# Keeping the gelu derivative of the last chunk in SBUF, and starting the FFN backward with that chunk

## The chip, the cores and the metric

The kernel runs on one core of a Trainium2 chip. Times are device microseconds (us) of one execution. A run is called slow when it took over 1.5% longer than the fastest run of the same kernel, otherwise fast.

A ratio is the mean time of one kernel's fast runs over that of the other's fast runs of the same rounds, so it isn't quite the ratio of the medians that stand beside it.

TensorE, VectorE, ScalarE, GpSimd and SyncE are PE, DVE, ACT, POOL and SP in the profile. PEld is TensorE's weight load. L12 is line 12 of the kernel, and the same statement has a number some 13 higher after the change.

## The reference

One transformer block and its gradients: 2048 tokens, width 512, FFN width 1792, 32 heads of 16 values. Attention looks at 8 positions, each 2 apart. Cut to what matters:

```python
h  = x + A_ref(layernorm(x), wqkv, wo)           # dilated window attention
h2 = h + gelu(layernorm(h) @ w1 + b1) @ w2 + b2  # tanh form of gelu
_out, _vjp = jax.vjp(_f, A_x, A_wqkv, A_wo, B_w1, B_b1, B_w2, B_b2)
return (_out, *_vjp(grad_out))                   # eight outputs
```

## The kernel before

The tokens are cut in four chunks of 512 (c = 0 to 3). The forward makes `u` (the input of gelu) and `s` (a sigmoid of it) in pairs of feature tiles, seven pairs a chunk, stores both to DRAM beside the result `g`, and the FFN backward loads them again to make the derivative `y`:

```python
# forward, for each chunk c and each of its seven pairs f2
z = ...; nc.scalar.activation(out=z[:], in_=u[:], func=ACT.Square)
...                                              # two VectorE operations on z
nc.scalar.activation(out=s[:], in_=z[:], func=ACT.Sigmoid, scale=2.0 * GC)
nc.vector.tensor_tensor(out=gt[:], in0=u[:], in1=s[:], op=ALU.mult)
for dd, t_ in ((x_d[c][r0:r1, :], u), (s_d[c][r0:r1, :], s), (g_d[...], gt)):
    pq.dma_start(out=dd.rearrange(...), in_=t_[:])      # pq is GpSimd's queue

# FFN backward of one chunk (b1_gg), for each pair
u = br2.tile(..., tag="bu", bufs=4); s = br2.tile(..., tag="bs", bufs=4)
...                                              # loads u and s on pq
nc.scalar.activation(out=y[:], in_=u[:], func=ACT.Square)
...                                              # five VectorE, one ScalarE operation: y
# psg = grad_out @ w2.T on TensorE; then gh = psg * y on VectorE
```

Behind the matmuls of one backward chunk runs the gradient of w2 as filler. Its transposed tiles `gtm` come from DRAM, 512 KB each, through two buffers.

`b_go(c)` turns the chunk's gradient through wo (TensorE, matmuls psgo), stores it as `go_r`, and `b_ga(c)` loads it as `go` and makes the gradient of the attention weights: products `pag` on VectorE, sums `ga` on TensorE, the results `gl` on VectorE. `b_sum` then makes the gradients of v, q and k from `r` (loads of `go_r`, `k_r` and `q_r`), with products `pb` on VectorE. Each engine gets its instructions in an order that is fixed when the kernel is built, and that isn't always the source's: in e2 below, loads of `r` go out at 506.1 us, before a store (527.2 us) that stands ahead of them in the source.

```python
for i in range(1, NC):                    # the i-th chunk of the backward
    ...                                   # b1_gg(i), with filler gw2
    if i == NC - 1:
        mix(b_go(0), none)
        b_ga(0)
    ...                                   # b1_gx(i), with filler gw2
    if i > 1:
        mix(b_go(i - 1), none)
b_ga(1)
mix(b_go(3), gw2)                         # the chunk that came last
...                                       # gb1r: the sum of grad b1, its store on SP
for c in range(NC):
    ...                                   # b_sum(c, 2), with filler grad w1
    if c + 2 < NC:
        b_ga(c + 2)
```

## Time and profile before

| | before |
|---|---|
| three runs known at first | 767.05, 771.17, 756.03 us |
| profiled execution: span, clock | 760.9 us, 0.937 |
| TensorE, VectorE, ScalarE, GpSimd busy | 83%, 73%, 52%, 29% |
| bytes moved by DMA | 170.91 MB |
| last g of the forward | 296.7 us |
| gb1r (FFN backward and grad w2 done) | 528.7 us |
| last gl (end of the last b_ga) | 597.3 us |

The last three rows are read from the view of one tile's instructions. It prints how often an instruction ran, its shortest, median and longest duration in ns, and the start of its first and last one in us. For the kernel before:

```profile
L784 DVE COPY gb1r<-ptg x1: 205/205/205, 528.7 to 528.7; 14x128 bf16<-14x128 bf16 x1
L731 DVE TENSOR_TENSOR gl<-attn,sp x8: 681/686/693, 517.2 to 597.3; 128x512 bf16<-128x512 bf16 x8
```

They are used as milestones: the same work must be done by then in every version. The remaining views of this kernel (busy times, stretches, waits, groups) stand in the prediction, with how to read them.

### The profile page before, as it was taken

To read this page: it belongs to the slowest core of one execution; us is meant where nothing else is said; L and a number is where in the kernel's file an instruction comes from. 1 tells how busy PE (TensorE), PEld (TensorE's weight loads), DVE (VectorE), ACT (ScalarE), POOL (GpSimd) and SP (SyncE) were. 2 spreads that over 40 slices of the span, in tenths; PEclk is the share of its full clock that TensorE was granted. 3 is DMA by queue.
4 is the path that set the end of the run, shared out by engine and by line. 5 is a ranking of instruction groups with operands and counts; after the bars stand their busy time and mean duration, and the time that the engine had idled before them with its cause. 6 is when DMAs were issued, how large, how long until landed. Compare 5 with 4: busy or idle time off the path is not lost. (4 is left out here: it accounts for less than half of the span.)

```text
span 760.9 us, 10214 instructions
## 1 busy us (share of the span) xinstructions
PE 629.8 (83%) x3552; PEld 263.9 (35%) x3618; DVE 556.3 (73%) x919; ACT 391.9 (52%) x545; POOL 219.5 (29%) x330
## 2 busy tenths in 40 slices
PE   2896478698795898966989898998898868999996
PEld 1441122233241333323444444443332323334342
DVE  5538879799758453563989898377988958898745
ACT  4662238759277374453778677552111323356443
POOL 4343333435244266441342433312101201000100
PEclk9997789699697899987999999999999989999999
DMA  8587897858677599999797785837987698975462
GB/s 222 167 296 201 225 332 249 292 201 270 245 218 238 150 251 273 272 244 146 161 207 160 192 190 146 254 104 242 400 236 286 189 335 280 327 260 175 154 124 69
DMA packets 112769, 170.91 MB, mean 225 GB/s; under 512 B 69549, under 2 KB 77582, under 8 KB 112718
## 3 DMA queue, kind: packets, MB, share of 16 engines
q1 hardware_dynamic: 80092, 79.45, 39.4%
q0 software_dynamic: 25856, 84.52, 35.0%
q10 hardware_dynamic: 6770, 6.30, 2.8%
q8 instruction: 28, 0.46, 0.3%
q14 instruction: 23, 0.19, 0.1%
HBM read 94.64 MB, written 60.38 MB: 204 GB/s over the span
## 5 line engine op out<-in xcount | busy, mean ns | idle before, releaser
L328 DVE TENSOR_TENSOR pb<-ba,r 128x2048 bf16<-128x2048 bf16 x96 | 112.3, 1220 | 15.2 <-PE pss L333 15.1
L631 PE MATMUL psw<-gout,gtm 128*128 128x512 bf16 x201 | 51.6, 391 | 22.1 <-DMA gtm<-g_d 11.5
L471 PE MATMUL psf<-ln2T,w 128*128 128x512 bf16 x217 | 57.5, 394 | 10.3 <-ACT u L473 9.4
L749 PE MATMUL psw<-h1tm,ln2a 128*128 128x512 bf16 (+1 forms) x248 | 54.6, 352 | 7.9 <-ACT ow L752 6.0
L494 PE MATMUL ps<-w,g 128*128 128x512 bf16 x217 | 54.6, 382 | 3.6 <-DVE g L481 3.4
L685 PE MATMUL psx<-w1T,gh 128*128 128x512 bf16 x214 | 51.3, 379 | 0.9 <-DVE luf L617 0.7
L664 DVE CUSTOM_DVE_ANT_0 gh<-psg,by 128x512 bf16<-128x512 f32 x54 | 36.1, 685 | 13.6 <-PE psg L662 11.9
L650 ACT ACTIVATE by<-bu 128x1024 bf16<-128x1024 bf16 x28 | 29.7, 1059 | 30.1 <-DVE gb1p L664 25.1
L311 DVE TENSOR_TENSOR pag<-go,bv 128x2048 bf16<-128x2048 bf16 x32 | 38.0, 1219 | 6.4 <-PE ga L318 3.4
L369 ACT CAST qkv<-psq 128x512 bf16<-128x512 f32 x48 | 27.6, 586 | 28.1 <-PE psq L367 28.1
L328 DVE TENSOR_TENSOR pbo<-a,v 128x2048 bf16<-128x2048 bf16 x32 | 38.1, 1216 | 5.3 <-DMA a<-at_r 4.2
L662 PE MATMUL psg<-goutT,w2T 128*128 128x512 bf16 x160 | 41.5, 379 | 0.6 <-DVE gb1p L664 0.2
L473 ACT ACTIVATE u<-psf,b1c 128x512 bf16<-128x512 f32 x56 | 36.4, 681 | 7.7 <-PE psf L471 3.4
L631 PEld LDWEIGHTS <-gtm 128*128 128x128 bf16 x208 | 20.4, 100 | 48.9 <-issue 15.8
L479 ACT ACTIVATE s<-z 128x1024 bf16<-128x1024 bf16 x28 | 29.4, 1058 | 14.4 <-DMA s_d<-s 8.6
L673 ACT COPY th<-pth 128x1024 bf16<-128x1024 bf16 x27 | 27.1, 1004 | 18.2 <-PE pth L671 15.1
L749 PEld LDWEIGHTS <-ln2a 128*128 128x128 bf16 x256 | 22.6, 97 | 36.9 <-issue 20.9
L675 POOL DMA_DIRECT2D h1tm_d<-th x27 | 20.6, 764 | 48.5 <-ACT th L673 46.7
L471 PEld LDWEIGHTS <-w 128*128 128x128 bf16 x224 | 20.7, 100 | 39.0 <-issue 20.8
L481 DVE TENSOR_TENSOR g<-u,s 128x1024 bf16<-128x1024 bf16 x28 | 19.1, 688 | 19.7 <-ACT s L479 19.7
L333 PE MATMUL pss<-pb,sel 128*32 128x512 bf16 x384 | 30.8, 389 | 2.6 <-DVE pb L328 2.4
L842 PE MATMUL psy<-wqkvT,gT 128*128 128x512 bf16 x125 | 32.0, 383 | 0.4
(196 smaller groups left out, 1340.8 us busy)
## 6 DMA issues: line engine op xcount, KB each, us to landing
v<-v_r SPq DMA_DIRECT2D x16, 576.0 KB, 7.7
r<-go_r SPq DMA_DIRECT2D x16, 576.0 KB, 8.6
r<-k_r SPq DMA_DIRECT2D x16, 576.0 KB, 8.3
r<-q_r SPq DMA_DIRECT2D x16, 576.0 KB, 4.9
x_d<-u POOLq DMA_DIRECT2D x28, 256.0 KB, 4.4
s_d<-s POOLq DMA_DIRECT2D x28, 256.0 KB, 4.7
g_d<-g POOLq DMA_DIRECT2D x28, 256.0 KB, 4.2
bu<-x_d POOLq DMA_DIRECT2D x28, 256.0 KB, 4.9
```

Of the source, the lines that this page charges most:

```text
L311: nc.vector.tensor_tensor(out=pr[:], in0=_ap(q_ap, [q_ap.ap[0], [P, 2], [0, W], [1, P]]), in1=_ap(k_ap, [k_ap.ap[0], [P, 2], [-DIL * P, W] ...
L328: last = nc.vector.tensor_tensor(out=pr[:], in0=_ap(a_ap, [a_ap.ap[0], [2 * H, CJ], [0, Q4], [1, H]], off=wh * H + (4 * H * wh if sg else 0)),
L333: mm = nc.tensor.matmul(ps[PR * n:PR * n + PR, :], lhsT=sel4[:], rhs=prs[wh][:, TC * n:TC * n + TC, :, :].rearrange("p j d h -> p (j d h)" ...
L471: nc.tensor.matmul(ps[:], lhsT=w1[0][:, dc, ft * P:(ft + 1) * P], rhs=ln2T[:, dc, :], start=(dc == 0), stop=(dc == DC - 1))
L473: nc.scalar.activation(out=u[:, i, :], in_=ps[:], func=ACT.Identity, bias=b1c[:, ft:ft + 1], scale=1.0)
L494: nc.tensor.matmul(ps[:], lhsT=gs[ft // 2][:, ft % 2, j * P:(j + 1) * P], rhs=w2[0][:, ft, :], start=(ft == 0), stop=False)
L631: nc.tensor.matmul(ps[:], lhsT=gtm[:, t, :], rhs=gout[t // TC][:, t % TC, :], start=(t == 0), stop=(t == NT - 1))
L662: nc.tensor.matmul(ps[:], lhsT=w2T[:, dc, ft * P:(ft + 1) * P], rhs=gT[:, dc, :], start=(dc == 0), stop=(dc == DC - 1))
L664: nc.vector.tensor_tensor_reduce(out=t1[:, k2, :], in0=ps[:], in1=y[:, k2, :], scale=1.0, scalar=0.0, op0=ALU.mult, op1=ALU.add, accum_out ...
L685: nc.tensor.matmul(ps[:], lhsT=t1s[ft // 2][:, ft % 2, j * P:(j + 1) * P], rhs=w1T[:, ft, :], start=(ft == 0), stop=(ft == FT - 1))
L749: nc.tensor.matmul(ps[:, 0:nf * P], lhsT=ln2a[:, t // TC, t % TC, dc * P:(dc + 1) * P], rhs=tmx[:, t, 0:nf * P], start=(t == 0), stop=(t = ...
L842: nc.tensor.matmul(ps[:], lhsT=gT[sel][:, g, j * P:(j + 1) * P], rhs=wqkvT[:, sel * G + g, :], start=(n == 0), stop=(n == NJ - 1))
```

## The change

The intent: the last chunk's `u` and `s` are still in SBUF at the end of the forward. If its `y` is made there and kept (in the buffers of `bu` and `bs`, seven of eight), that chunk's stores, loads and squares fall away, and its backward can begin at once. For that the backward must begin with chunk 3. The core of the diff:

```diff
+    def dgelu(y, u, s, t):        # five operations, as before in the backward
 ...
+            if c == 3:
+                tag = "bu" if f2 < 4 else "bs"
+                y = ys[f2] = br2.tile([P, 2, CH], BF16, name=f"y{c}_{f2}", tag=tag, bufs=4)
+                nc.vector.tensor_scalar(out=y[:], in0=z[:], scalar1=6.0 * GC * GK, scalar2=2.0 * GC, ...)
 ...
+            if c == 3:
+                dgelu(y, u, s, z)
-            for dd, t_ in ((x_d[c][r0:r1, :], u), (s_d[c][r0:r1, :], s), (g_d[...], gt)):
+            for dd, t_ in ((x_d[c][r0:r1, :], u), (s_d[c][r0:r1, :], s), (g_d[...], gt))[2 if c == 3 else 0:]:
 ...
-    b1_order = (0, 1, 2, 3)
+    b1_order = (3, 0, 1, 2)
 ...
+    ...                               # w1T_load and the set-up of the backward, moved up
+    mix(f_ffn1(3), f_ffn2(2))         # moved down behind them
 ...
+            if c in yc:
+                y = ...                   # the kept tile: no load, no chain
+            else:
                 ...                       # as before
 ...
         if i > 1:
-            mix(b_go(i - 1), none)
+            mix(b_go(3 if i == 2 else 1), none)
     b_ga(1)
-    mix(b_go(3), gw2)
+    mix(b_go(2), gw2)
```

Since y borrows buffers of the backward, the set-up of the backward (its pools, the first load of grad_out, the load of w1T) now stands ahead of the last forward chunk in the source. The order of `b_ga` (0, 1, 2, 3) is not changed.

More of the change, by code (lines that the diff above doesn't have):

```diff
@@ L459 @@
     GB = 12
-    gts = {}
+    gts, ys = {}, {}
+    def dgelu(y, u, s, t):
+        nc.vector.tensor_tensor(out=y[:], in0=y[:], in1=u[:], op=ALU.mult)
+        nc.scalar.activation(out=t[:], in_=s[:], func=ACT.Identity, bias=one_t[:], scale=-1.0)
+        nc.vector.tensor_tensor(out=y[:], in0=y[:], in1=t[:], op=ALU.mult)
+        nc.vector.tensor_scalar(out=y[:], in0=y[:], scalar1=1.0, scalar2=None, op0=ALU.add)
+        nc.vector.tensor_tensor(out=y[:], in0=y[:], in1=s[:], op=ALU.mult)
     def f_ffn1(c):
@@ L475, in f_ffn1 @@
             nc.scalar.activation(out=z[:], in_=u[:], func=ACT.Square)
+            if c == 3:
+                tag = "bu" if f2 < 4 else "bs"
+                y = ys[f2] = br2.tile([P, 2, CH], BF16, name=f"y{c}_{f2}", tag=tag, bufs=4)
+                nc.vector.tensor_scalar(out=y[:], in0=z[:], scalar1=6.0 * GC * GK, scalar2=2.0 * GC, op0=ALU.mult, op1=ALU.add)
             nc.vector.tensor_scalar(out=z[:], in0=z[:], scalar1=GK, scalar2=1.0, op0=ALU.mult, op1=ALU.add)
@@ L482, in f_ffn1 @@
             gts[c].append(gt)
+            if c == 3:
+                dgelu(y, u, s, z)
             r0, r1 = 2 * f2 * P, (2 * f2 + 2) * P
-            for dd, t_ in ((x_d[c][r0:r1, :], u), (s_d[c][r0:r1, :], s), (g_d[r0:r1, c * CH:(c + 1) * CH], gt)):
+            for dd, t_ in ((x_d[c][r0:r1, :], u), (s_d[c][r0:r1, :], s), (g_d[r0:r1, c * CH:(c + 1) * CH], gt))[2 if c == 3 else 0:]:
                 pq.dma_start(out=dd.rearrange("(i p) t -> p i t", p=P), in_=t_[:])
@@ L569 @@
     f_h(3)
-    mix(f_ffn1(3), f_ffn2(2))
     fr.release()
-    fl.release()
     br1 = pool("br1", 1, side="right")
-    b1_order = (0, 1, 2, 3)
+    b1_order = (3, 0, 1, 2)
     gout, goutT = {}, {}
@@ L599, in make_goutT @@
             to_T(gout[c], goutT[c], f"e{c}", "T")
+    w1T_load = sync.dma_start_transpose(out=w1T[:], in_=B_w1[:, :])
+    gate(w1T_load, ("r", 3))
+    mix(f_ffn1(3), f_ffn2(2))
+    fl.release()
     make_goutT(0)
-    gate(sync.dma_start_transpose(out=w1T[:], in_=B_w1[:, :]), ("r", 3))
     for c in b1_order[1:]:
@@ L643, in b1_gg @@
         for f2 in range(FT // 2):
-            u = br2.tile([P, 2, CH], BF16, name=f"bu{c}_{f2}", tag="bu", bufs=4)
-            s = br2.tile([P, 2, CH], BF16, name=f"bs{c}_{f2}", tag="bs", bufs=4)
-            for t_, d_t in ((u, x_d), (s, s_d)):
-                dd = d_t[c][2 * f2 * P:(2 * f2 + 2) * P, :]
-                pq.dma_start(out=t_[:], in_=dd.rearrange("(i p) t -> p i t", p=P))
-            y = br2.tile([P, 2, CH], BF16, name=f"by{c}_{f2}", tag="by", bufs=2)
-            mark["y", i, f2] = nc.scalar.activation(out=y[:], in_=u[:], func=ACT.Square)
-            nc.vector.tensor_scalar(out=y[:], in0=y[:], scalar1=6.0 * GC * GK, scalar2=2.0 * GC, op0=ALU.mult, op1=ALU.add)
-            nc.vector.tensor_tensor(out=y[:], in0=y[:], in1=u[:], op=ALU.mult)
-            nc.scalar.activation(out=u[:], in_=s[:], func=ACT.Identity, bias=one_t[:], scale=-1.0)
-            nc.vector.tensor_tensor(out=y[:], in0=y[:], in1=u[:], op=ALU.mult)
-            nc.vector.tensor_scalar(out=y[:], in0=y[:], scalar1=1.0, scalar2=None, op0=ALU.add)
-            nc.vector.tensor_tensor(out=y[:], in0=y[:], in1=s[:], op=ALU.mult)
+            if c in yc:
+                y = yc.pop(c)[f2] if f2 == FT // 2 - 1 else yc[c][f2]
+            else:
+                u = br2.tile([P, 2, CH], BF16, name=f"bu{c}_{f2}", tag="bu", bufs=4)
+                s = br2.tile([P, 2, CH], BF16, name=f"bs{c}_{f2}", tag="bs", bufs=4)
+                for t_, d_t in ((u, x_d), (s, s_d)):
+                    dd = d_t[c][2 * f2 * P:(2 * f2 + 2) * P, :]
+                    pq.dma_start(out=t_[:], in_=dd.rearrange("(i p) t -> p i t", p=P))
+                y = br2.tile([P, 2, CH], BF16, name=f"by{c}_{f2}", tag="by", bufs=2)
+                mark["y", i, f2] = nc.scalar.activation(out=y[:], in_=u[:], func=ACT.Square)
+                nc.vector.tensor_scalar(out=y[:], in0=y[:], scalar1=6.0 * GC * GK, scalar2=2.0 * GC, op0=ALU.mult, op1=ALU.add)
+                dgelu(y, u, s, u)
             t1 = get(br1, [P, 2, CH], BF16, f"gh1{c}_{f2}", "gh1", 8)
@@ L691 @@
     gw2 = gw2_gen()
-    gh1 = {}
+    gh1, yc = {}, {3: ys}
     mix(b1_gg(0), f_ffn2(3))
```

## The prediction

> **What bounds the kernel now.** I read the page first, then the busy time by stretch, then the waits and the ordered list of each engine between 262 and 362 us, where the changed code runs, and last the chain that ended last.
>
> The page's busy times say which engine has least room, and its slices say when:
>
> ```profile
> PE 629.8 (83%) x3552; PEld 263.9 (35%) x3618; DVE 556.3 (73%) x919; ACT 391.9 (52%) x545; POOL 219.5 (29%) x330
> ...
> PE   2896478698795898966989898998898868999996
> ```
>
> A slice is 19 us. TensorE is busiest, and from the fifteenth slice on (266 us) it is 80 to 90% busy nearly everywhere. The dip in the changed region is the pair "66" in the eighteenth and nineteenth slice, 323 to 361 us. The chain that ended last covers only the final 60 us and is matmuls (psy, psq) almost alone. So a microsecond saved in the middle reaches the end if it is a microsecond of TensorE idleness; work taken off another engine is worth nothing by itself. The table by stretch, cut at the stages, shows how much idleness there is:
>
> ```profile
> core 0: us, PE busy (x) PEld busy (x) DVE busy (x) ACT busy (x) POOL busy (x), PEclk, DMA share, GB/s
> ...
> 262.00:298.00 36.00, 30.57 (x151) 13.41 (x152) 14.39 (x24) 25.37 (x31) 18.44 (x28) 1.00 1.06 267
> 298.00:335.00 37.00, 34.72 (x187) 15.57 (x190) 21.12 (x44) 17.57 (x19) 18.83 (x30) 1.00 0.96 259
> 335.00:347.00 12.00, 0.52 (x3) 0.03 (x1) 4.48 (x10) 4.15 (x4) 5.08 (x7) 0.62 1.20 177
> 347.00:362.00 15.00, 13.42 (x62) 5.96 (x64) 6.57 (x16) 5.64 (x6) 3.41 (x5) 0.85 0.98 163
> 362.00:402.00 40.00, 37.24 (x223) 18.38 (x227) 36.05 (x87) 29.96 (x39) 15.05 (x21) 1.00 0.86 182
> ```
>
> 262 to 298 is the forward of chunk 3 (its gelu), 298 to 362 the FFN backward of the first chunk with what remains of the forward's second matmul, and then one backward chunk per 40 us. TensorE idles 5.4 + 2.3 + 11.5 + 1.6 = 20.8 us in these 100, and at a grant of 0.85 the 13.42 us after the gap cost about 13.42 x 0.15 = 2.0 us more. Each later chunk of 40 us idles under 4 us, with VectorE at 36 of 40. So the ceiling of the change is some 23 us. The waits of that window name the causes:
>
> ```profile
> PE psw L631 <- DMA gtm<-g_d: 11.5, 1, 11.5
> DVE g L481 <- ACT s L479: 12.7, 7, 3.6
> ACT s L479 <- DMA s_d<-s: 5.4, 3, 3.7
> ACT by L650 <- DMA bu<-x_d: 4.9, 1, 4.9
> PE ps L494 <- DVE g L481: 3.4, 2, 2.7
> ```
>
> The big one is one wait of 11.5 us for gtm, the transposing load of stored gelu values for the gradient of w2. It is not a wait for u or s. The others are the s buffers held by their stores (5.4) and the reload of u (4.9), of which TensorE feels 3.4.
>
> **What the Trainium skill says.** Four places bear on this. "VectorE: DVE Perf Modes", section on the perf-mode tier table: a bf16 tensor_scalar in SBUF may reach 4 elements per cycle, tensor_tensor 2. The trace agrees in direction: at 128x1024, 0.43 us against 0.69. "ScalarE: Activation LUTs", section "What ACT_TABLE_LOAD costs": every function runs at the same rate, and a pointer operand adds about 93 ns. The trace: Square 1.057 us, the 1-s Identity with its bias tile 1.149, a difference of 92 ns. "DMA: Bandwidth & Descriptors", section "Issuing engines are not separate DMA queues": transfers from all issuers interleave on the same 16 engines. The trace fits: gtm's time to landing runs from 4.5 to 29.2 us (median 10.0), long where GpSimd's loads are thick. "TensorE: Matmul & The Clock Gate", section "HAM oscillation": a long wait for a DMA drops the clock and the next matmuls start slow. The trace agrees: 0.62 and 0.85 around the gap, 1.00 before it.
>
> **The change, part by part.** Durations are from the rows of these instructions:
>
> ```profile
> L650 ACT ACTIVATE by<-bu 128x1024 bf16<-128x1024 bf16 x28 | 29.7, 1059 | 30.1 <-DVE gb1p L664 25.1
> L479 ACT ACTIVATE s<-z 128x1024 bf16<-128x1024 bf16 x28 | 29.4, 1058 | 14.4 <-DMA s_d<-s 8.6
> L481 DVE TENSOR_TENSOR g<-u,s 128x1024 bf16<-128x1024 bf16 x28 | 19.1, 688 | 19.7 <-ACT s L479 19.7
> ...
> x_d<-u POOLq DMA_DIRECT2D x28, 256.0 KB, 4.4
> s_d<-s POOLq DMA_DIRECT2D x28, 256.0 KB, 4.7
> ```
>
> Removed: 7 squares on ScalarE, 7 x 1.06 = 7.4 us; 14 stores and 14 loads of 256 KB, 28 x 0.262 = 7.3 MB of 170.9 MB (4.3%), and on GpSimd 28 x 0.72 = 20 us of issuing. TensorE loses and gains nothing. Added: nothing; VectorE makes the same five operations per pair of feature tiles, 0.43 + 0.69 + 0.69 + 0.43 + 0.69 = 2.93 us, x 7 = 20.5 us.
>
> Moved: those 20.5 us of VectorE and 7 x 1.15 = 8.0 us of ScalarE go from the backward of the first chunk into the forward of chunk 3. There VectorE has 14.4 us in 36 now, so it will have 34.9, and ScalarE 25.4 + 8.0 = 33.4. Both still fit, but only just: per pair ScalarE has 2 x 0.68 + 1.06 + 1.06 + 1.15 = 4.63 us and VectorE 1.80 + 2.93 = 4.73, in order, with z and s held longer in two buffers each. In exchange the waits for stores (5.4 + 1.2 for u) go. I choose 2 us longer for this stage: the last g comes at about 298 instead of 296. TensorE has other work meanwhile: the second matmul of chunk 2, the transposes of grad_out, and now also the first backward matmuls, whose y is ready one by one.
>
> Then the backward of chunk 3 needs no load and no chain: per pair VectorE only has two multiplies from PSUM, 2 x (0.685 + 0.08) = 1.53 us, x 7 = 10.7 us instead of 31.2. Between 298 and 362 TensorE did 48.7 us of work in 64. With everything it needs in SBUF, except gtm, the same work could end near 350.
>
> The gtm wait is what decides. Between 298 and 347 the queues moved 11.7 MB, of which the 20 issues of bu and bs are 5.2. In the new kernel the first chunk has none; what is loaded there is the next chunk, released as y tiles are consumed, since y borrows those buffers. I count 14 loads before the new stage's end instead of 24, and 3.7 MB less stored just before. I take two thirds of the 11.5 + 2.0 us as recovered: 9 us. Of the 3.4 us of waiting for g I take half back, 1.7, and pay 2 for the longer stage.
>
> The order 3, 0, 1, 2 puts chunk 2's attention-side gradient (b_go) last. Its values are now read by b_ga(2), two b_ga later; in the trace of before the load of that go stands at 540 us and the last b_go matmuls end near 521, so the 4 us of a store fit between. I charge 1 us. Sum: -9 - 1.7 + 2 + 1 = about -8 us.
>
> **The rivals.**
> *A. The idle moves.* gtm could still be late, because the static order puts the same transposes ahead of matmuls that are ready. For it: the wait was for a transpose, not for bu or bs, and DMA moved only 177 GB/s during the gap at a share of 1.20, so these transposes are slow by themselves. Against: the gap lies right behind a burst of loads (q0 had 63.5% of 16 engines' span from 298 to 347). Then the gain is 0 to 3 us: 762 to 765.
> *B. VectorE becomes the bound of the chunk-3 forward.* At 4.73 us a pair, with hand-overs to ScalarE and back inside each pair, it might take 5.5 us: 38.5 us plus 2.8 for the outputs, some 5 us longer. For it: both engines near 95% of the stage and in order. Against: TensorE has backward work to fill with. This costs 3 to 5 us of the gain: 760 to 764.
> *C. The whole dip closes.* Nothing waits for DMA, the clock stays at 1.00, and nearly all of the 23 us comes back: 742 to 747. For it: 31 us of VectorE chain leave a 64 us stage. Against: TensorE was busy for 34.7 of the 37 us before the gap, so the chain itself hardly held it up.
>
> **Range and chances.** The three times of before are 767.05, 771.17 and 756.03, with a mean of 764.8; the profiled run took 762.7. I take 765 as the base, subtract 8, and say 757.0. The base alone is uncertain by some 5 us, the gain between rival A and C by 7 or so either way: 744 to 768. Faster by over 2% needs 15 us, which is between my sum and rival C: 0.22. Slower by 15 us would need a new wait that nothing in the profile shows: 0.03. Within 2%: 0.75.
>
> **What would show it right or wrong.** Right: the row of the waits for gtm falls from 11.5 us to under 4; TensorE's idleness from 262 us to the end of the first chunk's psg falls from 20.8 to about 12; the granted clock stays at 1.00 there; bu and bs have 21 loads each, x_d and s_d 21 stores each; the squares at the backward line are 21; DMA bytes are near 163.6 MB; the forward of chunk 3 has VectorE at 34 to 36 us and lasts 36 to 40. The later chunks keep 40 us each. Wrong: the gtm wait stays (A), VectorE's idle before g grows and the last g comes after 303 us (B), or a new wait for go appears near 525 to 550 us. If the first-chunk stage shortens and the end doesn't move, the idea that TensorE's idleness there reaches the end has fallen.

## More of the kernel before

Every experiment ran on one chip together with the unchanged kernel before. The experiments ran on four chips (8, 9, 3 and 15), so most comparisons here are made within one chip.

A version that keeps y but leaves the backward in the order 0, 1, 2, 3 doesn't build: the y of chunk 3 would need its own room beside `bu` and `bs`, and their pool then 34 KB per partition where 23.56 are left.

## The result

| | before, same chip | after |
|---|---|---|
| median (range), runs | 761.54 (754.13 to 771.17), 4 | 757.07 (756.47 to 758.47), 4 |
| ratio of the fast runs, 95% interval | | 1.003 (1.0006 to 1.0054) |
| profiled execution: span, clock | 760.9 us, 0.937 | 754.9 us, 0.942 |

Among fast runs there was no gain. The forecast time, 757.0, was met to 0.1 us, but the forecast gain of 8 us was measured from a base of 765, and two of the four runs of before (756.03, 754.13) were as quick as the kernel after. What the change visibly did in these runs is narrow the spread. The three times that both unchanged kernels ran together:

| chip | before: median (range) | after: median (range) | ratio of fast runs |
|---|---|---|---|
| first comparison | 761.54 (754.13 to 771.17) | 757.07 (756.47 to 758.47) | 1.003 (1.0006 to 1.0054) |
| 8 | 761.91 (755.99 to 774.98) | 755.45 (754.55 to 759.15) | 0.9931 (0.9878 to 0.9984) |
| 15 | 762.79 (753.65 to 770.26) | 754.37 (751.84 to 757.03) | 0.9946 (0.9853 to 1.004) |

So among fast runs the change is worth between 0.3% lost and 0.7% gained, and 4 to 8 us in the medians.

### The profile after

The page's busy times, TensorE's slices (19 us each) and the bytes:

```profile
PE 632.7 (84%) x3552; PEld 263.6 (35%) x3618; DVE 555.9 (74%) x919; ACT 384.6 (51%) x538; POOL 199.6 (26%) x302
...
PE   2896578699695798989999999977887977999996
...
DMA packets 110529, 163.57 MB, mean 217 GB/s; under 512 B 69101, under 2 KB 77134, under 8 KB 110478
```

The "66" of the eighteenth and nineteenth slice is now "89", and a softer dip "77887" has appeared further on, from the twenty-seventh slice (491 us). In both profiles 3552 of 3618 matmuls are recorded, so busy sums that lie close together should not be pressed. The same stretches as in the prediction (span of the stretch, then PE, PEld, DVE, ACT and POOL busy with counts, granted clock, DMA share, GB/s):

```profile
262.00:298.00 36.00, 33.41 (x177) 15.45 (x179) 29.88 (x59) 33.27 (x40) 14.17 (x24) 1.00 0.96 218
298.00:335.00 37.00, 33.31 (x187) 15.63 (x190) 23.19 (x56) 16.88 (x20) 16.13 (x23) 0.96 0.70 233
335.00:347.00 12.00, 11.95 (x69) 5.29 (x68) 8.66 (x21) 7.97 (x12) 0.77 (x1) 0.98 0.05 15
347.00:362.00 15.00, 14.75 (x83) 6.28 (x83) 14.34 (x35) 10.94 (x13) 8.61 (x12) 1.00 1.02 242
...
442.00:482.00 40.00, 38.07 (x227) 17.73 (x231) 24.13 (x49) 23.00 (x35) 9.73 (x14) 1.00 0.66 176
482.00:525.00 43.00, 34.66 (x189) 15.03 (x190) 25.24 (x30) 7.13 (x13) 7.71 (x13) 0.92 0.76 216
```

TensorE's idleness from 262 to 362 us fell from 20.8 to 2.6 + 3.7 + 0.05 + 0.25 = 6.6 us. The loads of gtm aren't faster in this window, they have left it: the list of SyncE's queue has none between these two lines (start, duration of the group).

```profile
280.70 2.56 SPq L642 DMA_TRANSPOSE gtm<-g_d  x1
...
351.40 64.99 SPq L642 DMA_TRANSPOSE gtm<-g_d  x6
```

In the kernel before, loads of gtm go out at 313.5 and from 317.8 us on, and the filler that reads them, a few matmuls up to 298 us apart, goes on at 309.7; after the change it goes on at 349.2 us only.

VectorE now works only 24 of 40 us in the last backward chunk and 25 of 43 behind it, where TensorE idles 8.3 us. For comparison, those last two stretches in the kernel before:

```profile
442.00:482.00 40.00, 36.28 (x212) 17.78 (x218) 34.62 (x81) 29.39 (x40) 12.73 (x18) 1.00 0.60 158
482.00:525.00 43.00, 40.51 (x232) 18.07 (x235) 25.71 (x41) 21.00 (x34) 9.00 (x15) 1.00 0.64 196
```

What VectorE waits for between 480 and 600 us in the kernel after (us in total, times, longest):

```profile
DVE pag L311 <- PE ga L318: 10.5, 3, 6.8
DVE pag L311 <- DMA go<-go_r: 10.5, 2, 7.3
DVE pb L328 <- DMA r<-go_r: 5.5, 2, 5.1
```

In the kernel before, the wait for go is 3.1 us there and that for r does not appear:

```profile
DVE pag L311 <- PE ga L318: 3.4, 3, 2.1
DVE pag L311 <- DMA go<-go_r: 3.1, 2, 1.6
```

And the milestones after:

```profile
L797 DVE COPY gb1r<-ptg x1: 200/200/200, 518.7 to 518.7; 14x128 bf16<-14x128 bf16 x1
L744 DVE TENSOR_TENSOR gl<-attn,sp x8: 680/684/693, 488.0 to 591.2; 128x512 bf16<-128x512 bf16 x8
```

gb1r comes 10.0 us earlier than in the profile of before, the last gl 6.1, the end of the span 6.0. So 4 us of what the middle gained are lost between gb1r and the last gl. From there to the end both take the same (163.6 and 163.7 us).

### The profile page after: what moved, and what is told of

It reads as the page before. It is cut to its first block, busy times and chain, and to the rows that moved or that the text cites. A ratio compares the mean times of both kernels' runs of the same rounds, so it can differ in the third digit from the quotient of the medians.

```text
span 754.9 us, 10122 instructions
## 1 busy us (share of the span) xinstructions
PE 632.7 (84%) x3552; PEld 263.6 (35%) x3618; DVE 555.9 (74%) x919; ACT 384.6 (51%) x538; POOL 199.6 (26%) x302
## 5 line engine op out<-in xcount | busy, mean ns | idle before, releaser
L762 PE MATMUL psw<-h1tm,ln2a 128*128 128x512 bf16 (+1 forms) x248 | 56.8, 364 | 9.2 <-ACT ow L765 6.2
L311 DVE TENSOR_TENSOR pag<-go,bv 128x2048 bf16<-128x2048 bf16 x32 | 38.0, 1218 | 21.0 <-PE ga L318 10.5
L688 POOL DMA_DIRECT2D h1tm_d<-th x27 | 20.6, 764 | 56.6 <-ACT th L686 56.5
L765 ACT CAST ow<-psw 128x512 bf16<-128x512 f32 (+1 forms) x16 | 8.5, 532 | 48.2 <-PE psw L762 42.0
L827 ACT ACTIVATE gt<-pss 128x512 bf16<-128x512 f32 x32 | 19.1, 597 | 27.2 <-PE pss L333 26.6
L667 ACT ACTIVATE by<-bu 128x1024 bf16<-128x1024 bf16 x21 | 22.1, 1054 | 20.8 <-DVE gb1p L677 18.2
L882 PE MATMUL psq<-gt,ln1a 128*128 128x512 bf16 x124 | 30.6, 380 | 0.5 <-ACT owq L886 0.2
```

What stands on the lines that cost most here:

```text
L311: nc.vector.tensor_tensor(out=pr[:], in0=_ap(q_ap, [q_ap.ap[0], [P, 2], [0, W], [1, P]]), in1=_ap(k_ap, [k_ap.ap[0], [P, 2], [-DIL * P, W] ...
L762: nc.tensor.matmul(ps[:, 0:nf * P], lhsT=ln2a[:, t // TC, t % TC, dc * P:(dc + 1) * P], rhs=tmx[:, t, 0:nf * P], start=(t == 0), stop=(t = ...
L882: nc.tensor.matmul(ps[:], lhsT=ln1a[:, t // TC, t % TC, dc * P:(dc + 1) * P], rhs=gts[sel, t // TC][:, t % TC, :], start=(t == 0), stop=(t ...
```

## The experiments

Sixteen kernels ran, all with correct results. Theory A in the expectations: the middle gains, and a part is lost behind it. Theory B: only the spread of before. The milestones of the profiled executions, in us:

| kernel | last g | gb1r | last gl | last pb | end of span | gl to end | pb to end |
|---|---|---|---|---|---|---|---|
| before (the profile predicted from) | 296.7 | 528.7 | 597.3 | 718.6 | 760.9 | 163.6 | 42.3 |
| e0, before again | 297.3 | 521.2 | 589.7 | 709.6 | 751.8 | 162.1 | 42.2 |
| after | 298.3 | 518.7 | 591.2 | 712.6 | 754.9 | 163.7 | 42.3 |
| e2, order alone | 290.7 | 526.9 | 599.4 | 721.1 | 763.7 | 164.3 | 42.6 |
| e3, after with go early | 298.9 | 515.7 | 575.5 | 698.6 | 741.2 | 165.7 | 42.6 |
| e5, order alone with go early | 297.8 | 525.0 | 599.6 | 722.0 | 764.0 | 164.4 | 42.0 |
| e6, before with go early | 296.8 | 522.7 | 579.3 | 703.2 | 745.9 | 166.6 | 42.7 |
| e11, after with dead stores | 312.8 | 532.0 | 605.6 | 727.9 | 770.6 | 165.0 | 42.7 |
| e15, after, third time | 294.8 | 514.9 | 587.1 | 708.0 | 750.4 | 163.3 | 42.4 |
| e12, after with dead loads | 294.9 | 522.3 | 594.8 | 719.5 | 762.0 | 167.2 | 42.5 |
| e14, go early and b_ga(3) earlier | 297.5 | 520.3 | 557.0 | 694.0 | 736.4 | 179.4 | 42.4 |

The last pb is VectorE's last product in b_sum. The end follows it by 42.0 to 42.7 us in every row, wherever the middle ended. e2 and e5 were profiled in their quickest execution (765.4 and 765.8 us of medians of 773 and 775), so their rows show less than their medians cost.

### The kernels themselves, again

**e1_after_again** is the kernel after, unchanged, with five rounds, on chip 8.

> The changed kernel once more, to have it and the kernel before timed in the same rounds. Both theories: 756 to 759 us. Theory A (the change gains in the middle and loses it again in the attention part of the backward): the runs of before that are fast lie within 3 us of it, and a fast profile of before would show a shorter gtm wait. Theory B (the 6 us between the two profiles are the spread of the kernel before, and the change is worth nothing anywhere): the runs of before scatter from 754 to 771 again and the changed kernel's do not.

Measured: 755.45 (754.55 to 759.15), ratio 0.9931 (0.9878 to 0.9984). The kernel after is steady, and the fast runs of before are a little slower here.

**e0_before_again** is the kernel before, unchanged, for a second trace, on chip 9.

> The kernel before, unchanged, for a second profile and its scatter. In the five profiles so far the time from the last gl (end of b_ga(3)) to the end was 163.6 to 165.7 us. Theory A, now: the end is the last gl plus 164 us, in every kernel here, so what counts is when VectorE ends b_ga(3). Expected here too, with 756 to 775 us in all and a wait of some length for gtm in the first backward chunk. If the sum fails by more than 4 us, theory A is wrong.

Measured: 759.52 (753.6 to 773.32), and the profiled run was the quickest, 753.6. Its trace is what the comparison needed. The stretches that hold the dip in the first profile of before are full here, in the same kernel:

```profile
335.00:347.00 12.00, 11.34 (x70) 5.63 (x70) 9.89 (x24) 7.93 (x9) 5.58 (x8) 1.00 1.10 323
347.00:362.00 15.00, 14.04 (x87) 6.89 (x86) 12.97 (x33) 11.87 (x17) 6.16 (x9) 1.00 0.75 221
```

and TensorE's waits for gtm between 262 and 362 us are one of 2.6 us, where the first profile had 11.5:

```profile
PE psw L631 <- DMA gtm<-g_d: 2.6, 1, 2.6
```

The whole-kernel time from issue to landing of gtm was 6.1, 8.1 and 14.7 us here (shortest, median, longest), and 4.5, 10.0 and 29.2 in the first profile (4.7, 6.8 and 7.4 in the kernel after, where these loads go out at other times). So the wait that the prediction made its largest term belongs to one of the two traced executions of the kernel before and not to the other, and both count as fast (762.7 and 753.6 us). In the other kernels' traces TensorE's longest wait for gtm is 5.0 us, wherever it falls. TensorE's idleness from 262 to 362 us is 10.0 us in e0, not 20.8. Against e0 the change gains 2.5 us up to gb1r (521.2 to 518.7), then loses 4.0, as gb1r to the last gl takes 72.5 instead of 68.5. The quickest trace of the kernel after (e15) reaches gb1r 6.3 us ahead of e0, and the end 1.4; it takes 72.2 from gb1r to the last gl. That agrees with a ratio near 1.

### The order without the kept y

**e2_order_alone** takes only the order from the change; u and s of chunk 3 are stored and loaded as before.

```diff
-    b1_order = (0, 1, 2, 3)
+    b1_order = (3, 0, 1, 2)
-            mix(b_go(i - 1), none)
+            mix(b_go(3 if i == 2 else 1), none)
-    mix(b_go(3), gw2)
+    mix(b_go(2), gw2)
```

> The kernel before with only the order of the chunks 3, 0, 1, 2 and of the b_go calls as in the changed kernel; u and s of chunk 3 still go out to DRAM and come back. Theory A: the order costs 3 to 6 us behind 480 us (late go for b_ga), and the reload right behind the store costs more at the first chunk: 759 to 766. Theory B: order is neutral, 754 to 758, as the fast runs of before.

Measured: 773.05 (765.44 to 776.6) against 761.91 for before and 755.45 for after on the same chip, ratio to before 1.015 (1.009 to 1.0211). The order alone costs 11 us, and keeping y under that order gains 17.6. The prediction had charged the order with 1. By the milestones the order costs 5.7 us up to gb1r (against e0) and 4.0 behind it; keeping y gains 8.2 back up to gb1r and nothing behind it (72.5 both times). These traces hold only 8.8 of the 17.6 us, since e2 was profiled in its quickest execution; its other five took 771.6 us or more. No gtm wait is among TensorE's waits between 262 and 362 us in e2, so in this execution the loss isn't the dip.

### Making go earlier

**e3_go_early** is the kernel after, in which the go of chunks 0 and 1 is made one place earlier and that of chunk 3, which b_ga needs last, later.

```diff
-            mix(b_go(0), none)                       # before the last chunk's gx
+            mix(b_go(1), none)
-            mix(b_go(3 if i == 2 else 1), none)
+            mix(b_go(0 if i == 2 else 3), none)
```

> The changed kernel with the b_go calls in the order 0, 1, 3, 2 instead of 3, 0, 1, 2, so that b_ga(0) and b_ga(1) read a go stored long before. Theory A: the wait of VectorE for go at b_ga(1) (3.2 us, and the 6.8 us behind it) goes, and 2 to 5 us with it: 752 to 755. Theory B, or a tail bound by other loads: 756 to 758 as the changed kernel.

Measured: 742.02 (736.48 to 745.04), ratio to before 0.9745 (0.9692 to 0.9799): faster, and 13.4 us below the kernel after on the same chip. b_ga(0) can run in the last backward chunk, where VectorE had stood idle, and between 480 and 600 us the waits for go, for r and for the sums ga shrink; a new one of 18.1 us stands in front of gb1r. Its stretch, and VectorE's waits:

```profile
442.00:482.00 40.00, 38.45 (x222) 16.78 (x225) 34.81 (x62) 20.86 (x31) 9.77 (x14) 1.00 0.73 214
```

```profile
DVE gb1r L797 <- PE ptg L795: 18.1, 1, 18.1
DVE pag L311 <- PE ga L318: 4.7, 3, 2.2
...
DVE pag L311 <- DMA go<-go_r: 0.9, 1, 0.9
DVE pb L328 <- DMA r<-go_r: 0.7, 2, 0.5
```

VectorE's 24.13 us in that stretch have become 34.81, go's wait went from 10.5 to 0.9 us, and r's from 5.5 to 0.7. gb1r moved by 3.0 us only, the last gl by 15.7, the span by 13.7. TensorE's work is the same.

How an early first b_ga helps the later ones can be read from SyncE's queue. The operands of b_ga, go and bv, have one buffer each, so the loads for the next b_ga go out only when the products of the one before are through. In the kernel after, b_ga(1) ends its products at 514.4 us, the load of the go for b_ga(2) goes out at 522.3 (on SyncE's queue the store of gb1r and the first loads of r are still ahead of it), and SyncE waits 3.1 and 15.2 us for VectorE's `pag` before such loads. In e3, b_ga(1) is through at 493.0 us; the load goes out at 507.8, now held by the store of that go (5.4 us). No version with two buffers was run.

**e16_go_early_again** and **e15_after_third** are the same two kernels together on chip 15.

> The version with go early, unchanged, for a comparison on this chip: theory A (it gains some 13 us over the kernel after, whichever the chip) 738 to 745; if it comes at 750 or more, the gain of the first run was the chip's.

> The kernel after the change, unchanged, for a comparison on this chip: median 754 to 758 in every theory, its range within 5 us.

Measured: 742.28 (739.94 to 745.05) and 754.37 (751.84 to 757.03). The means of the fast runs are 742.39 and 754.40, a ratio of 0.984. The gain of some 12 us is not one chip's.

**e7_go_as_before** is the kernel after with b_go(1) in the place that it had before the change and b_go(3) later: the order 1, 0, 3, 2 instead of 3, 0, 1, 2.

```diff
-            mix(b_go(3 if i == 2 else 1), none)
+            mix(b_go(1 if i == 2 else 3), none)
```

> The changed kernel with b_go(1) before the last chunk and b_go(0) behind it, exactly as the kernel before has them, and b_go(3) and b_go(2) last. Theory A, with the late b_go(1) as the whole loss: 743 to 747. If most of the gain of early go comes from b_go(0), which here is as late as in the changed kernel: 751 to 756.

Measured: 760.49 (756.73 to 764.11) on chip 9, ratio to before 0.9956 (0.9891 to 1.0021), no better than the kernel after. VectorE's waits for go between 480 and 600 us are 16.9 us. It isn't enough that b_go(1) is early; what helped in e3, which differs from e7 by the exchange of these two calls alone, is that b_go(0), which the first b_ga reads, comes before the last backward chunk.

**e5_order_go_early** is the order alone (e2) with the go order of e3, so without the kept y.

```diff
-            mix(b_go(3 if i == 2 else 1), none)      # and b_go(0) above it is b_go(1)
+            mix(b_go(0 if i == 2 else 3), none)
```

> The kernel before with the chunk order 3, 0, 1, 2 and the b_go calls in the order 0, 1, 3, 2, and no y kept. Together with the order alone (773), the changed kernel (755 to 757) and the same with early go (742) this is the fourth corner of a square. Theory A: the two parts add, 773 - 13 = 758 to 762, and keeping y is worth 16 to 20 us with either order of b_go. If keeping y pays only where go is late, this comes near 745.

Measured: 775.38 (765.77 to 778.19), ratio 1.0131 (1.0035 to 1.0227). That is a miss: the early go gained nothing here. VectorE's waits between 480 and 600 us say what came in its place:

```profile
DVE pb L328 <- DMA r<-go_r: 10.5, 1, 10.5
DVE pag L311 <- DMA go<-go_r: 6.9, 1, 6.9
DVE gb1r L784 <- PE ptg L782: 6.6, 1, 6.6
```

On SyncE's queue the loads of r stand behind the store of gb1r, and gb1r is late here. The ordered list of that queue (start, duration):

```profile
525.23 0.39 SPq L785 DMA_DIRECT2D out_dram<-gb1r  x1
525.72 3.24 SPq L282 DMA_DIRECT2D r<-go_r  x4
```

In e3 the same loads go out from 516.4 us on. In e2 the same four loads went out from 506.1 us on, ahead of that store, and VectorE had no wait for r; its waits for go were 12.7 us. So against e2 the wait for go shrank by 5.8 us and one for r took its place. Against e3 the last gl comes 24.1 us later: 9.3 of them stand at gb1r already, the other 14.8 arise behind it, where the waits for r and go are 17.4 us instead of 1.6. Neither theory had that, and no edit has tested it.

**e6_before_go** is the kernel before with only its b_go(0) and b_go(1) exchanged, so without anything of the change.

```diff
-            mix(b_go(0), none)
+            mix(b_go(1), none)
-            mix(b_go(i - 1), none)
+            mix(b_go(0 if i == 2 else 2), none)
```

> The kernel before, chunk order 0, 1, 2, 3, with b_go(0) put before the last backward chunk instead of behind it (b_go in the order 0, 1, 2, 3). If the gain of early go has nothing to do with the change, the kernel before gains as much: 746 to 752. If before is bound by TensorE until 525 us, it gains under 4 us: 757 to 764.

Measured: 747.69 in the profiled run, then 757.14 and four from 766.62 to 769.05: a median of 767.17 against 768.83 on that chip, ratio 0.9853 (0.9718 to 0.9988) from two fast runs. It can be as quick as 748 us, but keeps the spread of before. In the trace of that quickest run, gb1r to the last gl takes 56.6 us instead of 68.5 (e0), so in this execution the early go works in that stage without the change too; the four slow runs have no trace. How much it is worth in all stays unclear.

### What gates VectorE behind 497 us

**e4_gb1_off_sp** is the kernel after with the store of gb1r on ScalarE's queue, so that r is not behind it.

```diff
-    sync.dma_start(out=out_5.rearrange("(ft p) -> ft p", p=P), in_=gb1r[:])
+    nc.scalar.dma_start(out=out_5.rearrange("(ft p) -> ft p", p=P), in_=gb1r[:])
```

> The changed kernel with the small store of the gradient of b1 issued by ScalarE instead of SyncE, where it holds up the loads of r for the first b_sum (issued at 519.4, right behind it; VectorE then idles 5.2 us for r). Theory A: that idle falls under 2 us and 1 to 3 us come back: 754 to 756. If these loads are held by something else (buffers, the go store), nothing moves: 756 to 758.

Measured: 756.84 (748.83 to 758.31) against 755.45 for the kernel after: the same. The loads of r went out at 516.4 instead of 519.4 us, and the wait for r fell from 5.5 to 4.7 us only. In the kernel after that queue place is no limit by itself.

**e8_gb1_late** is e3 with the whole sum of grad b1 moved behind grad w1; **e9_after_gb1_late** does the same to the kernel after.

```diff
-    gb1s = ...                # reduction, transpose, gb1r, store: nine lines
 ...                           # the b_sum loop with grad w1
     mix(wg, none)
+    gb1s = ...                # the same nine lines
```

> The version with go made early (e3_go_early), and the sum of grad b1 (its reduction, its transpose on TensorE, its copy gb1r and its store) moved behind grad w1. In e3 VectorE idled 18.1 us in front of gb1r (497.5 to 515.7), in program order, before it could go on with b_ga(2) and b_ga(3). Theory A (the end is VectorE's last b_ga plus about 164 us): that wait goes, the last gl comes some 8 to 18 us earlier than e3's 575.5, so at 558 to 568, unless b_ga(2) then waits for go instead, and the end comes at 724 to 735. Rival (TensorE's own work sets the end of this part, VectorE only fills in): the wait goes and others take its place, gl within 4 us of 575, the end at 738 to 746.

> The kernel after the change with only the sum of grad b1 moved behind grad w1; the order of b_go as it is there. Theory A, second part (what holds VectorE back between 480 and 525 us in the kernel after is b_go(0) coming late, not gb1r in front of b_ga(2)): the span stays within 5 us of 755, the waits for go (7.3 us at 569, 3.2 us at 496 us) stay. Rival (gb1r is the gate in both): last gl by 8 us or more earlier than 591, the end at 747 or less.

Measured: 742.35 (737.37 to 750.79) and 752.52 (751.85 to 759.77) on chip 3. Both are what e3 and the kernel after give on other chips. In e9 the waits for go stay (8.8 us). In e8 the 18.1 us wait in front of gb1r went, as expected, but a wait for go of the same length took its place (its profile fell on its slow run, 750.79 us, so its milestones aren't used):

```profile
DVE pag L311 <- DMA go<-go_r: 18.8, 1, 18.8
```

So in e3 gb1r only hid it: once the first two b_ga are early, b_ga(2) needs the go of chunk 2, the chunk that the new order puts last. The rival's account (another wait takes its place) and its time came; that TensorE's work is the cause isn't shown, and the last gl, at 581.2 us in that slow run, doesn't test its 575.

**e14_ga3_early** follows from that. It is e3 with b_go(3) made before the last chunk, since chunk 3 is the first of the backward, and with b_ga(3) put in front, so that the chunk whose go comes last is also used last.

```diff
-        if i > 1:
-            mix(b_go(0 if i == 2 else 3), none)
+        if i == 2:
+            mix(b_go(3), none)
+            mix(b_go(0), none)
     b_ga(1)
+    b_ga(3)
 ...
-        if c + 2 < NC:
-            b_ga(c + 2)
+        if c == 0:
+            b_ga(2)
```

> The version with go early, and further: b_go(3) is made before the last backward chunk (chunk 3 was the first, so its gradient is long there), b_ga(3) stands before b_go(2), and b_ga(2) is the last. VectorE's wait in front of gb1r (18.1 us) is to be filled with b_ga(3). Theory A (the end is VectorE's last b_ga plus 162 to 167 us): the last gl at 558 to 566 instead of 575.5, the end at 723 to 733. Rival 1 (the chain after the last b_ga then has a new limit, the transfers or TensorE): last gl earlier by 8 us or more, but more than 170 us from there to the end, 733 to 742. Rival 2 (b_go(3) earlier holds TensorE's last chunk up by as much, so that go(2) comes no earlier): last gl within 3 us of 575, the end at 738 to 744.

Measured: 740.27 (737.7 to 743.05), ratio to before 0.9761 (0.9669 to 0.9853), and mean 740.32 beside 742.39 of e16 on the same chip, with ranges that overlap. It is the quickest version, though its lead of 2 us over e3's edit isn't resolved. The last gl came at 557.0 us, better than expected:

```profile
L744 DVE TENSOR_TENSOR gl<-attn,sp x8: 678/684/692, 466.4 to 557.0; 128x512 bf16<-128x512 bf16 x8
```

But from there to the end it took 179.4 us, which is rival 1. So "the end is the last gl plus some 164 us", which held in every other trace (162 to 168 us), held only as long as the b_ga were the last limit. The products pb begin no earlier than in e3 (520.4 and 520.9 us) though there is one b_ga less among them, and the last comes 4.6 us earlier (694.0 and 698.6). From 560 to 600 us VectorE works 29.11 us where it worked 36.38 in e3, at a DMA share of 0.97 (0.88 in e3), and its waits between 480 and 620 us for TensorE's sums of pb are 9.9 us (6.5 in e3):

```profile
DVE pb L328 <- PE pss L333: 9.9, 8, 2.5
```

Which of these is the new limit, no run has told apart.

### What the removed transfers are worth

**e11_dead_stores** is the kernel after that still stores u and s of chunk 3, unread.

```diff
-            for dd, t_ in (...)[2 if c == 3 else 0:]:
+            for dd, t_ in (...):
```

> The kernel after the change, but u and s of the last chunk are still written to DRAM (16 stores of 256 KB's worth that nobody reads). Both theories: the stores of the last forward chunk lie beside TensorE work, so the end stays within 2 us of the kernel after (753 to 757). If instead it comes 4 us or more later, or the first transposed loads come late, the removed stores are a part of the gain that the prediction did not count.

Measured: 771.4 (769.85 to 772.41) on chip 3, some 16 us above the kernel after (755.45 and 754.37 on its two chips). The expectation failed. The last g came at 312.8 instead of 298.3 us. Between 240 and 315 us ScalarE, and between 240 and 365 us TensorE, waited as follows:

```profile
ACT s L491 <- DMA s_d<-s: 8.0, 1, 8.0
```

```profile
PE psw L645 <- DMA gout<-in_grad_out_dram: 11.5, 1, 11.5
```

and GpSimd, between 262 and 312 us:

```profile
POOL x_d L499 <- DMA x_d<-u: 8.7, 1, 8.7
```

The two buffers of s are held by their stores while the chain of y stands in the same stage. GpSimd waited 8.7 us for an earlier store of u to land before it issued the next, and the load of grad_out behind it went out at 301.77 us. TensorE, in order, stood 11.5 us before one filler matmul that needed grad_out.

**e10_dead_loads** put the 14 loads back, dead, into the tile tag `by`.

```diff
+  for n_, d_t in enumerate((x_d, s_d)):              # in the first backward chunk
+      w = br2.tile([P, 2, CH], BF16, name=f"dl{n_}_{f2}", tag="by", bufs=2)
+      pq.dma_start(out=w[:], in_=d_t[c - 1][...])
```

> The kernel after the change, with the loads that it saved put back as dead ones: 14 loads of 256 KB (u and s of the chunk before) into a tile that nothing reads, in the first chunk of the backward. No VectorE or ScalarE work is put back. Theory A (part of the saving is the loads: the transposed loads gtm then find the queues empty): a wait for gtm comes back on TensorE between 335 and 362 us, 3 to 12 us, and gb1r comes 2 to 8 us later, the end 2 to 8 us later (757 to 763). Rival (the saving is VectorE's and ScalarE's work for y, the transfers were hidden): no wait over 3 us for gtm there, end within 2 us of 755.

Measured: 766.21 (762.73 to 772.3). This experiment was badly made: the next chunk's y uses that tag, and ScalarE waited 15.2 us for a dead load to leave it. It measured its own wait.

**e12_dead_loads_own** puts them where the kernel before has them, in `bu` and `bs`.

```diff
-      w = br2.tile(..., tag="by", bufs=2)
+      w = br2.tile(..., tag=("bu", "bs")[n_], bufs=4)
```

> The kernel after the change, with 14 dead loads of 256 KB (u and s of the chunk before) in the first backward chunk, now in the buffers bu and bs that the kernel before has for them and that nothing reads. Theory A (the loads themselves cost: they stand before the transposed loads in the DMA engines): gtm waits of 3 us or more on TensorE between 335 and 362 us, gb1r 2 to 8 us later than 518.7, the end at 757 to 763. Rival (loads are hidden; what the change pays for is VectorE's and ScalarE's work and the stores): gb1r within 2 us, the end at 753 to 757.

Measured: 769.1 (763.83 to 770.86) beside 754.37 of the kernel after on chip 15: 14 us slower by the means of the fast runs (768.22 and 754.40). Between 295 and 365 us TensorE has no wait for gtm, but no load of gtm goes out between 276.9 and 354.9 us either, so theory A's reason could not show. The next chunk's loads of u begin at 310.9 us (295.2 in e15), and ScalarE waits for them in that stretch:

```profile
ACT by L670 <- DMA bu<-x_d: 12.2, 2, 7.6
```

gb1r comes 7.4 us later than in e15 and the end 11.6. So without loads of its own the first backward chunk serves as a head start for the loads of the second. But this edit too measures waits of its own: y holds seven of these eight buffers, which it doesn't in the kernel before, and GpSimd waited 12.1 us for dead loads to land before it could issue the next. What the loads alone cost is not separated. Dead stores and dead loads each cost 14 to 16 us, nearly the whole 17.6 that keeping y is worth under this order. The two costs don't add up to the difference between e2 and after; in these runs the saving appears only when both are gone.

Two edits never ran because they don't fit in SBUF: dead loads in tiles of their own (their pool takes 24 KB per partition of 23.56 left), and a third gtm buffer in the kernel before (a pool of 26 KB where 23.06 are left), which would have tested the dip directly.

## Why the prediction was right or wrong

**The dip closes: right, but not for the reason given.** No wait for gtm is left between 262 and 362 us, TensorE's idleness there fell to 6.6 us (12 had been forecast), and the clock stayed at 0.96 or above. With 14.2 of 20.8 us gone, this region is nearer to rival C than to the sum; the end is not. The reason given was that gtm would find fewer transfers ahead of it. That was not put to the test: the new build issues no load of gtm between 280.7 and 351.4 us and gives TensorE matmuls psg and psx there instead. So rival A didn't come about either, as the order that it feared had changed. Over the whole execution TensorE waits 2.5 us for gtm after the change, 2.6 in e0, 11.5 in the profile predicted from.

**The longer forward: right, by way of the stores.** The last g came at 298.3 us (forecast 298), ScalarE worked 33.27 us in that stretch (33.4), VectorE 29.88 (34.9). Rival B fell. But e11 shows that the 2 us charged hold only because the stores went: with them the same stage ends 14.5 us later. The prediction had named the waits for stores that go (5.4 + 1.2 us); the experiment puts them higher. Part of it comes by a path that it didn't have, GpSimd's queue and the load of grad_out.

**"A microsecond saved in the middle reaches the end if it is a microsecond of TensorE idleness": this step failed.** Of 10.0 us at gb1r 6.0 reached the end; between the quickest traces (e0 and e15) 1.4 of 6.3. And e3 took 13.7 us off the span with the same TensorE work, by letting VectorE begin b_ga(0) in the last backward chunk. In that part the limit is a chain through b_go, its store, its load and VectorE's b_ga, and behind it VectorE's pb (the end is the last pb plus 42.0 to 42.7 us in the eleven traces of the table), not TensorE's total. The prediction's own test, the stage shorter and the end unmoved, came true in part.

**"I charge 1 us" for the order: mis-sized.** It costs 11 us in the medians (e2). The new waits for go came, at 496 and 569 us rather than at 525 to 550. But they aren't for chunk 2. What the prediction worked out for b_ga(2) holds in the kernel after: the stores of that go are issued by 498.3 us, its load goes out at 522.3, and VectorE doesn't wait for it. The waits are those of b_ga(1) (3.2 us) and b_ga(3) (7.3 us), whose stores of go were issued by 481.3 and 432.8 us and whose loads only at 489.2 and 557.0, when the b_ga before had left the single buffer (488.0 and 551.5 us); the second load also stood behind the transposing load of wqkvT (548.7 us) on SyncE's queue. The step looked at one chunk's go, not at the row of four b_ga through one buffer. Only when b_ga(0) and b_ga(1) come early does b_ga(2) wait for chunk 2 (18.8 us in e8). e14, which uses that chunk last, brings the last gl some 18 us earlier than e3 and e16. Which of these waits make up the 11 us of e2 is not shown.

**"I take two thirds of the 11.5 + 2.0 us as recovered: 9 us": this step failed.** It took a wait of one execution for a cost of the kernel. In the quick execution of before (e0) that wait is 2.6 us, and the change gains 2.5 us up to gb1r. The two traces of before differ by 9.1 us in the span and 7.5 at gb1r. Why gtm landed after 29.2 us in that execution isn't settled.

**The base of 765 us.** It was the mean of three runs of a spread that reaches from 753.6 to 775. The kernel after, measured at 754 to 757, is 8 us below that base, so 757.0 came out right. Against the fast runs it is from 0.3% worse to 0.7% better. The hit is luck: it is of the base, not a proof of the mechanism. By the medians keeping y gains 17.6 us under the new order (the sum had 8.7) and the order costs 11 (the sum had 1), which largely cancels, and the dip was one execution's.

**What stays open:** what makes up the 17.6 us of keeping y; why the spread is smaller after the change; why the early go gains 12 to 13 us with the kept y, nothing in e5, and an unclear amount in e6. That the wait for r took the place of that for go in e5 is read from its waits and its queue, and was not tested by a further edit.

## What to carry to other kernels

Take two or three traces of the kernel before, and see whether the wait that is to be removed is in the quick ones; the gain against those is what a comparison of fast runs will show. When a change reorders chunks, follow who reads each chunk's result downstream, and reorder those readers too: here that was worth more (12 to 13 us, with y kept) than the change itself. When a wait is gone, look whether the work that waited still stands there; here it had moved some 38 us on. A milestone per stage, with its distance to the next, shows at once in which stage a gain was given back.

## What the Trainium skill lacked or had wrong

- "DMA: Bandwidth & Descriptors", section "Latency and other measured facts": it gives 261 GB/s as effective bandwidth of a transposing DMA whose middle dimension isn't contiguous, and more where it is. Here transposing loads of 512 KB beside other traffic landed after 10.0 us in the median of one execution and 8.1 of another, so at about 52 and 65 GB/s if queueing is counted in (an estimate: 524,288 bytes over the time to landing), and with up to 29.2 us in the first. The section has no figure for such loads beside other traffic.
- No page that was found says how far the runs of one unchanged kernel on one core lie apart. Here it was 753.6 to 775 us for the kernel before, and 752 to 759 for the kernel after.
